# Bursts of three score tiles, a new order of MLP units, transposed constants and earlier first scores in a fused attention and MLP kernel

## The chip, the cores and the metric

The kernel runs on one core of a Trainium2 chip. The metric is the device time of one execution in microseconds (us), as a median over several runs. A difference of less than 2% counts as "same" in the verdicts, so most of what follows is about differences that need many rounds on the same chip, or the trace, to be seen at all. A "cold" stretch is one in which the trace shows a granted TensorE clock of 0.50.

## The reference

For 8 batches of 12 heads, 448 positions and head size 64: q and k are normalized by their root mean square and scaled by gains, then softmax attention; its output, 3584 tokens of 768, goes through an MLP with a leaky activation whose slope `alpha` differs per hidden unit.

```python
q_n, k_n = rmsnorm(q, g_q), rmsnorm(k, g_k)
scores = np.matmul(q_n, k_n.transpose(0, 1, 3, 2)) / sqrt(64)
attn = softmax(scores)                      # over keys
x = matmul(attn, v) -> (3584, 768)
h = x @ w_in                                # 768 x 2048
g = np.maximum(h, 0.0) + alpha * np.minimum(h, 0.0)
out = g @ w_out                             # 2048 x 768
```

## The kernel before

The kernel is scheduled by hand: the order in which instructions are written is the order on each engine. A batch is three blocks `y` of four heads, a block is seven score tiles `j`. The engines are called as in the profile: PE is TensorE, DVE is VectorE, ACT is ScalarE, POOL is GpSimd. One block's life:

- POOL squares q and k (`square`), DVE sums the squares (`reduce`), ACT makes 1/root (`root`), POOL scales (`scale`; DVE for the first blocks), PE transposes both and DVE copies them out of PSUM, the memory into which PE writes (`turn`);
- PE makes score tiles (`score`), ACT their exponential (`soft`), PE sums over keys with ones (`den`), ACT inverts by a logarithm and an exponential (`log`, `invert`), PE multiplies with v (`attv`) and DVE multiplies by the inverse into `xT`;
- the MLP of a batch is 16 "up" units of six matmuls and about seven "down" units of sixteen matmuls.

```python
def turn(y):
    ps = psa.tile([128, 2, 512], FP32, name="tps", tag="acc")     # one buffer, shared with den and attv
    ...  # 7 transposes of q, 7 of k, then one copy each
def attv(y):
    av = over_keys("av", y, lambda g, par, j: vv[...])            # 28 matmuls of 64x64, tag "acc"
    nc.vector.tensor_mul(out=xT[b][:, :, i, :], in0=av[:, :, :S], in1=rden[y])
def up(b, ft):
    hT = psf.tile([128, 512], FP32, name="hT", tag="mm")          # two buffers, shared with down
    ...  # six matmuls
    nc.scalar.activation(out=ah, in_=hT[:, :S], func=AF.Copy, scale=alpha_sb[:, ft : ft + 1])
    nc.vector.tensor_max(out=gT[:, ft, ds((b & 1) * S, S)], in0=hT[:, :S], in1=ah)
```

The program is a row of bursts. Each has two score tiles, possibly a denominator or an attention product, possibly a turn, then the MLP units that a planner put into its gap.

```python
    for b in range(1, B):
        at(J * G * b / 2 - 4, load_v, b)        # the second batch's v: burst 6
    ...
    for c in range(4):
        load_w_in(c)
        at(8 + 2 * c, load_w_out, c)            # bursts 8, 10, 12, 14
    ...
    for n in range(NB + 2):
        for f, a in prep.get(n, ()):
            f(*a)
        tiles = [divmod(m, J) for m in (2 * n, 2 * n + 1) if m < NG * J]
        for t in tiles:
            score(*t)
        if n in dens:
            den(dens[n])
        if n in avs:
            attv(avs[n])
        ...   # softmaxes, logarithm, root and scale of a later block
        if n in turns:
            turn(turns[n])
        for f, a in gaps[n]:                    # up and down units
            ...
        if n < first:
            spin(4 if plain else 1)             # matmuls that only fill PE's gaps
```

## Time and profile before

The median was 482.68 us of three runs.

| Stage of the trace | PE | ACT | What sets the pace |
|---|---|---|---|
| 0 to 14 us | filling matmuls | waits for q and k | the first loads |
| 14 to 50 us (head, no MLP work yet) | about 80% | about 85% | ACT |
| 50 to 450 us | about 97% | about 60% | PE |

In the profile, a busy share says when an engine had work and not how well it was used. Costs on PE are therefore read from the starts of successive groups in the timeline. The prediction shows the lines.

### The profile page before, as it was taken

Reading aid. Unit: us, or ns where it says so; the run is one execution under the profiler, and the core shown is the slowest. Engines: PE = TensorE matmul, PEld = TensorE weight load, DVE = VectorE, ACT = ScalarE, POOL = GpSimd, SP = SyncE. Lnnn points to the kernel's source line nnn. Section 1 sums busy time; section 2 is a strip of 40 time slices with the busy share of each in tenths; the row PEclk is TensorE's granted clock in tenths of the full one; section 3 lists DMA queues with packets and bytes.
Section 4 is the critical chain, followed back from the end, with each engine's and each line's share of the span. In section 5 each row is a group of like instructions: output and inputs, shape, how many; then the busy total and the mean of one; then the engine's idle time right before and its main releaser. Section 6 shows DMA issues by size and latency. Waiting matters only on the chain.

```text
span 480.6 us, 9494 instructions
## 1 busy us (share of the span) xinstructions
PE 451.2 (94%) x4074; PEld 234.9 (49%) x4074; DVE 217.3 (45%) x312; ACT 289.1 (60%) x399; POOL 167.0 (35%) x123
## 2 busy tenths in 40 slices
PE   7777899999999999999999999999999999999995
PEld 3243444555455445555545554554545554555463
DVE  2843564545354445355453454454462443334421
ACT  4788789567756657656755757548674558423300
POOL 4688734554253261451442351532623200000000
PEclk9799999999999999999999999999999999999998
DMA  7999997340705243431704434423401110111122
GB/s 197 200 266 221 241 209 135 110 110 3 167 1 143 77 116 53 117 100 38 167 0 110 110 100 69 110 54 90 92 1 35 34 34 1 34 34 33 34 65 67
DMA packets 32187, 45.46 MB, mean 95 GB/s; under 512 B 5008, under 2 KB 28560, under 8 KB 32144
## 3 DMA queue, kind: packets, MB, share of 16 engines
q1 hardware_dynamic: 19792, 32.13, 25.8%
q0 software_dynamic: 11776, 11.80, 15.7%
q10 hardware_dynamic: 576, 0.92, 0.7%
q8 instruction: 32, 0.52, 0.5%
q14 instruction: 11, 0.09, 0.1%
HBM read 45.62 MB, written 11.01 MB: 118 GB/s over the span
## 4 chain that ended last, share of the span: by engine, by line
PE 70%; ACT 12%; DVE 9%; issue 4%; POOL 3%; DMA 1%; SPq 0%; POOLq 0%; DVEq 0%; ACTq 0%
PE op L266 30%; PE hT L249 20%; ACT ah L257 6%; PE sc L189 6%; PE av L212 6%; PE dn L212 4%; DVE gT L258 4%; ACT expT L201 4%; DVE ss L133 3%; PE tps L166 2%; DMA nat<-in_k_dram 1%; POOL qs L150 1%; POOL sq L127 1%; ACT rden L227 1%; PE spin L289 1%
## 5 line engine op out<-in xcount | busy, mean ns | idle before, releaser
L201 ACT ACTIVATE expT<-sc,expb 128x896 f16<-128x896 f32 x168 | 160.4, 1004 | 51.2 <-PE sc L189 51.1
L249 PE MATMUL hT<-xT,w_in_sb 128*128 128x448 f16 x768 | 159.9, 352 | 8.1 <-DVE gT L258 6.5
L266 PE MATMUL op<-w_out_sb,gT 128*128 128x384 f16 x896 | 153.3, 326 | 1.7 <-DVE gT L258 1.7
L257 ACT ACTIVATE ah<-hT,alpha_sb 128x448 f16<-128x448 f32 x128 | 80.7, 635 | 97.2 <-PE hT L249 96.2
L258 DVE TENSOR_TENSOR gT<-hT,ah 128x448 f16<-128x448 f32 x128 | 79.5, 624 | 123.5 <-ACT ah L257 123.3
L150 POOL TENSOR_TENSOR qs<-nat,rr 128x896 f16<-128x896 f32 x45 | 75.0, 1688 | 127.9 <-ACT rr L145 104.1
L266 PEld LDWEIGHTS <-gT 128*128 128x128 f16 x896 | 85.2, 98 | 64.3 <-issue 11.2
L249 PEld LDWEIGHTS <-w_in_sb 128*128 128x128 f16 x768 | 72.4, 97 | 86.0 <-issue 26.2
L127 POOL TENSOR_TENSOR sq<-nat 128x896 f32<-128x896 f32 x44 | 72.9, 1677 | 85.4 <-DVE ss L133 85.4
L278 DVE COPY osb<-op 128x384 f32<-128x384 f32 x56 | 31.1, 556 | 86.5 <-PE op L266 86.5
L189 PE MATMUL sc<-qT,kT 64*64 64x448 f16 x672 | 51.7, 370 | 9.9 <-DVE kT L176 4.5
L133 DVE TENSOR_REDUCE ss<-sq 128x14 f32<-128x896 f32 x48 | 49.8, 1076 | 7.0 <-ACT sq L125 7.0
L240 DVE TENSOR_TENSOR xT<-av,rden 128x896 f16<-128x896 f32 x24 | 26.2, 1092 | 29.9 <-PE av L212 29.9
L212 PE MATMUL av<-expT,vt 64*64 64x448 f16 x672 | 36.0, 349 | 1.3 <-ACT rden L227 1.3
L212 PE MATMUL dn<-expT,ones 64*64 64x448 f16 x672 | 35.9, 349 | 0.0
L189 PEld LDWEIGHTS <-kT 64*64 64x64 f16 x672 | 13.9, 105 | 42.7 <-issue 32.2
L212 PEld LDWEIGHTS <-vt 64*64 64x64 f16 x672 | 20.0, 107 | 13.6 <-issue 2.4
L212 PEld LDWEIGHTS <-ones 64*64 64x64 f16 x672 | 19.9, 107 | 11.8 <-issue 0.3
L166 PE MATMUL tps<-ident,qs 128*128 128x128 f16 x336 | 23.3, 220 | 1.9 <-POOL qs L150 1.6
L227 ACT ACTIVATE rden<-dn 128x896 f32<-128x896 f32 x24 | 22.1, 921 | 3.5 <-PE dn L212 3.5
L166 PEld LDWEIGHTS <-qs 128*128 128x128 f16 x336 | 18.8, 98 | 10.8 <-issue 5.6
L232 ACT ACTIVATE rden<-rden 128x896 f32<-128x896 f32 x24 | 22.6, 943 | 0.3
(25 smaller groups left out, 98.9 us busy)
## 6 DMA issues: line engine op xcount, KB each, us to landing
out_dram<-osb SPq DMA_DIRECT2D x56, 192.0 KB, 2.7
nat<-in_q_dram SPq DMA_DIRECT2D x46, 224.0 KB, 3.8
nat<-in_k_dram SPq DMA_DIRECT2D x46, 224.0 KB, 4.6
vt<-in_v_dram POOLq DMA_DIRECT2D x16, 336.0 KB, 5.5
w_in_sb<-in_moe_w_in_dram POOLq DMA_DIRECT2D x4, 768.0 KB, 19.0
w_out_sb<-in_moe_w_out_dram POOLq DMA_DIRECT2D x4, 768.0 KB, 16.2
nat<-in_q_dram ACTq DMA_DIRECT2D x2, 224.0 KB, 5.2
nat<-in_k_dram ACTq DMA_DIRECT2D x2, 224.0 KB, 7.1
```

Of the source, the lines that this page charges most:

```text
L127: nc.gpsimd.tensor_mul(out=sqf, in0=src, in1=src)
L133: nc.vector.tensor_reduce(out=ss_t[y][:, "qk".index(nm)].rearrange("p h j -> p (h j)").unsqueeze(2), in_=sqs[y, nm], axis=AXIS_X, op=ALU.add,)
L150: eng.tensor_mul(out=t.rearrange("p j h d -> p h j d"), in0=nat[y, nm], in1=rr_t[y][:, "qk".index(nm)].unsqueeze(3).broadcast_to((128, 2, ...
L166: nc.tensor.transpose(tp[:, j, :], qs[y, nm][:, j].rearrange("p h d -> p (h d)"), ident)
L189: nc.tensor.matmul(out=sc[ds(64 * g, 64), par, :S], lhsT=kT[ds(64 * par, 64), g, j, :], rhs=qT[ds(64 * par, 64), g].rearrange("p j c -> p ...
L201: nc.scalar.activation(out=expT[y][:, j], in_=scs[y, j][:, :, :S], func=AF.Exp, scale=QK_SCALE, bias=expb[:, 0:1],)
L212: nc.tensor.matmul(out=acc[ds(64 * par, 64), g, :S], lhsT=weights(g, par, j), rhs=e[ds(64 * g, 64), j, par, :], start=(j == 0), stop=(j == ...
L249: nc.tensor.matmul(out=hT[:, :S], lhsT=w_in_sb[:, c, ts(ft, 128)], rhs=x[:, c, :], start=(c == 0), stop=(c == KM - 1),)
L257: nc.scalar.activation(out=ah, in_=hT[:, :S], func=AF.Copy, scale=alpha_sb[:, ft : ft + 1])
L258: nc.vector.tensor_max(out=gT[:, ft, ds((b & 1) * S, S)], in0=hT[:, :S], in1=ah)
L266: nc.tensor.matmul(out=op[:, :OH], lhsT=gT[:, ft, ts(t, 128)], rhs=w_out_sb[:, ft, ds(oh * OH, OH)], start=(ft == 0), stop=(ft == NF - 1),)
L278: nc.vector.tensor_copy(out=o[:, ds(oh * OH, OH)], in_=op[:, :OH])
```

## The change

The intent is to let PE change less often between score work and MLP work, to keep third MLP units in a row from waiting for PSUM, and to start the first scores earlier. The diff, cut to its core:

```diff
@@ constants: rows, then one PE transpose, in place of 4-byte loads @@
+    rows = cst.tile([NF + 2, 128], FP32, name="rows", tag="rows")
+    cols = cst.tile([128, NF + 2], FP32, name="cols", tag="cols")
+    alpha_sb = cols[:, :NF]
@@ load_qk: the second block's loads wait for ACT @@
+            if hold and nm == "q":
+                nc.scalar.copy(out=t[:, 0, 0, 0:1], in_=expb)
@@ square @@
-        sq = ld.tile([128, 2 * J, D], FP32, name="sq", tag="sq", bufs=2)
+        sq = ld.tile([128, 2 * J, D], FP32, name="sq", tag="sq", bufs=4)
@@ turn: own PSUM tile for the first k; layout (j, g, c) in place of (g, j, c) @@
+        ps2 = psf.tile([128, 512], FP32, name="tps2", tag="mm") if y == 0 else ps[:, 1]
-            t = att.tile([128, 2, J, 64], FP16, name=f"{nm}T", tag=f"{nm}T", bufs=3)
+            t = att.tile([128, J, 2, 64], FP16, name=f"{nm}T", tag=f"{nm}T", bufs=3)
@@ plan of the bursts @@
+        if len(dens) > len(avs):
+            avs[n] = len(avs)
+        elif len(dens) < NG and last_in.get(len(dens), n) < n:
+            dens[n] = len(dens)
+        wide = n in dens and dens[n] >= G or n in avs and avs[n] >= G - 1
+        count = min(3 if wide else 2, NG * J - m)
@@ loads and preparation @@
-        at(J * G * b / 2 - 4, load_v, b)
+        at(av_at[G * b] - 4, load_v, b)          # the second batch: burst 11
-        at(8 + 2 * c, load_w_out, c)
+        at(7 + c, load_w_out, c)
@@ units: a down may now open any burst; a burst with a turn has two units @@
-            free = n in avs or n in turns
+            free = True
+                short = n in turns and len(gaps[n]) < 2
@@ start: q's chain before k's; gains multiplied between @@
-    spin(34)
+    spin(22)
+    ct = psf.tile([128, 512], FP32, name="ct", tag="mm")
+    nc.tensor.transpose(ct[:, : NF + 2], rows, ident32[: NF + 2, : NF + 2])
+    spin(12)
@@ main loop @@
-        for t in tiles:
+        for t in tiles[:2]:
             score(*t)
 ...  # den or attv
+        for t in tiles[2:]:
+            score(*t)
+            soft(*t)
 ...
-        if n in turns:
-            turn(turns[n])
         for k, (f, a) in enumerate(gaps[n]):
 ...
+            if k == 0 and n in turns:
+                turn(turns[n])
-            spin(4 if plain else 1)
+            spin(4)
```

More of the change, by code (lines that the diff above doesn't have):

```diff
@@ L76 @@
     nc.vector.memset(idle, 0.0)
+    ident32 = cst.tile([32, 32], FP32, name="ident32", tag="ident32")
+    make_identity(nc, ident32)
+    rows = cst.tile([NF + 2, 128], FP32, name="rows", tag="rows")
+    cols = cst.tile([128, NF + 2], FP32, name="cols", tag="cols")
+    alpha_sb = cols[:, :NF]
     gain = cst.tile([128, 1], FP32, name="gain", tag="gain")
-    gk2 = cst.tile([128, 1], FP32, name="gk2", tag="gk2")
-    alpha_sb = cst.tile([128, NF], FP32, name="alpha_sb", tag="alpha_sb")
     w_in_sb = cst.tile([128, KM, DF], FP16, name="w_in_sb", tag="w_in_sb")
@@ L85, with load_qk @@
     SRC = {"q": q4, "k": k4}
-    def load_qk(y):
+    def load_qk(y, hold=False):
         b, i = divmod(y, G)
@@ L159, in turn @@
         ps = psa.tile([128, 2, 512], FP32, name="tps", tag="acc")
+        ps2 = psf.tile([128, 512], FP32, name="tps2", tag="mm") if y == 0 else ps[:, 1]
         tps = [
-            ps[:, n, : S].bitcast(FP16).rearrange("p (j c) -> p j c", j=J)
-            for n in range(2)
+            t[:, : S].bitcast(FP16).rearrange("p (j c) -> p j c", j=J)
+            for t in (ps[:, 0], ps2)
         ]
@@ L169, in turn @@
         for tp, nm in zip(tps, "qk"):
-            t = att.tile([128, 2, J, 64], FP16, name=f"{nm}T", tag=f"{nm}T", bufs=3)
-            o = t.rearrange("p g j c -> p j g c")
-            i4 = tp.rearrange("p j (g c) -> p j g c", g=2)
+            t = att.tile([128, J, 2, 64], FP16, name=f"{nm}T", tag=f"{nm}T", bufs=3)
+            o = t.rearrange("p j g c -> p j (g c)")
             if nm == "q":
-                nc.vector.tensor_copy(out=o, in_=i4)
+                nc.vector.tensor_copy(out=o, in_=tp)
             else:
                 nc.vector.tensor_scalar(
-                    out=o, in0=i4, scalar1=gain[:, 0:1], scalar2=None, op0=ALU.mult
+                    out=o, in0=tp, scalar1=gain[:, 0:1], scalar2=None, op0=ALU.mult
                 )
@@ L189, in score @@
                 nc.tensor.matmul(
-                    out=sc[ds(64 * g, 64), par, :S],
-                    lhsT=kT[ds(64 * par, 64), g, j, :],
-                    rhs=qT[ds(64 * par, 64), g].rearrange("p j c -> p (j c)"),
+                    out=sc[ds(64 * g, 64), par, :S].rearrange("p (j c) -> p j c", j=J),
+                    lhsT=kT[ds(64 * par, 64), j, g, :],
+                    rhs=qT[ds(64 * par, 64), :, g, :],
                     start=True,
@@ L291, in spin @@
                 )
-    NB = (NG * J + 1) // 2
-    def last(y):
-        return (J * y + J - 1) // 2
-    dens = {last(y) + 1: y for y in range(NG)}
-    avs = {last(y) + 2: y for y in range(NG)}
+    bursts, dens, avs, first_in, last_in = [], {}, {}, {}, {}
+    m = 0
+    while m < NG * J or len(avs) < NG:
+        n = len(bursts)
+        if len(dens) > len(avs):
[4 more added lines that the diff above has]
+        count = min(3 if wide else 2, NG * J - m)
+        bursts.append([divmod(m + c, J) for c in range(count)])
+        for y, j in bursts[n]:
+            first_in.setdefault(y, n)
+            if j == J - 1:
+                last_in[y] = n
+        m += count
+    NB = len(bursts)
+    den_at = {y: n for n, y in dens.items()}
+    av_at = {y: n for n, y in avs.items()}
     prep, post, roots = {}, {}, {}
@@ L309, in after @@
         post.setdefault(max(int(n), 0), []).append((f, a))
-    turn_at = [J * y // 2 - 1 for y in range(NG)]
-    turns = {n: y for y, n in enumerate(turn_at) if y}
+    turn_at = {
+        y: max(n for n in range(first_in[y]) if n not in dens) for y in range(1, NG)
+    }
+    turns = {n: y for y, n in turn_at.items()}
     jobs = {}
     for y in range(G, NG):
-        n = turn_at[y - 1] if y < G + 2 else last(y - G) + 2
-        at(n - 8, load_qk, y)
+        early = y < G + 2
+        n = turn_at[y - 1] if early else max(d for d in dens if d <= turn_at[y] - 2)
+        at(n - (8 if early else 5), load_qk, y)
         for nm in "qk":
             at(n - 2, square, y, nm)
-            if y < G + 2:
+            if early:
                 after(n, reduce, y, nm)
@@ L338 @@
         ]
-        tail = len(new) if b == B - 1 else 2 + odd
+        tail = len(new) if b == B - 1 else 2 if odd or b == 0 else 1
         periods.append((ups, carry, new[:tail]))
@@ L343, in cost @@
     def cost(n):
-        return 0.75 + (1.35 if n in dens or n in avs else 0.0) + (0.9 if n in turns else 0.0)
-    first = last(G - 1) + 2
-    gaps = [[] for _ in range(NB + 2)]
+        return (
+            0.31 + 0.19 * len(bursts[n])
+            + (1.35 if n in dens or n in avs else 0.0) + (0.9 if n in turns else 0.0)
+        )
+    first = av_at[G - 1]
+    gaps = [[] for _ in range(NB)]
     for b in range(B - 1):
-        lo = last(G * b + G - 1) + 2
-        hi = last(G * b + 2 * G - 1) + 2
+        lo, hi = av_at[G * b + G - 1], av_at[G * b + 2 * G - 1]
         ups, old, new = (list(u) for u in periods[b])
@@ L368 @@
                 ahead = 0.5 * (UP if ups else DOWN)
-                if n < hi - 1 and clock + ahead > per * (n - lo + 1):
+                short = n in turns and len(gaps[n]) < 2
+                if n < hi - 1 and not short and clock + ahead > per * (n - lo + 1):
                     break
@@ L381 @@
     nc.scalar.preload_act_table_set("natural_log_exp_and_others")
-    for g in range(2):
-        nc.gpsimd.dma_start(out=gain[ds(64 * g, 64)], in_=g_q.unsqueeze(1))
-        nc.gpsimd.dma_start(out=gk2[ds(64 * g, 64)], in_=g_k.unsqueeze(1))
-    load_qk(1)
+    nc.gpsimd.dma_start(out=rows[:NF], in_=moe_alpha.rearrange("(t p) -> t p", p=128))
+    for n, g in enumerate((g_q, g_k)):
+        for h in range(2):
+            nc.gpsimd.dma_start(
+                out=rows[NF + n : NF + n + 1, ds(64 * h, 64)], in_=g.unsqueeze(0)
+            )
+    load_qk(1, True)
     load_qk(2)
-    nc.sync.dma_start(out=alpha_sb, in_=moe_alpha.rearrange("(t p) -> p t", p=128))
-    spin(34)
+    spin(22)
+    ct = psf.tile([128, 512], FP32, name="ct", tag="mm")
+    nc.tensor.transpose(ct[:, : NF + 2], rows, ident32[: NF + 2, : NF + 2])
+    spin(12)
     for nm in "qk":
@@ L392 @@
         reduce(0, nm)
-    for nm in "qk":
         root(0, nm)
         scale(0, nm)
-    nc.vector.tensor_mul(out=gain, in0=gain, in1=gk2)
+        if nm == "q":
+            nc.vector.tensor_copy(out=cols, in_=ct[:, : NF + 2])
+            nc.vector.tensor_mul(
+                out=gain, in0=cols[:, NF : NF + 1], in1=cols[:, NF + 1 : NF + 2]
+            )
     turn(0)
@@ L411 @@
     roots[3] = 2
-    for n in range(NB + 2):
+    for n in range(NB):
         for f, a in prep.get(n, ()):
             f(*a)
-        tiles = [divmod(m, J) for m in (2 * n, 2 * n + 1) if m < NG * J]
-        for t in tiles:
+        tiles = bursts[n]
+        for t in tiles[:2]:
             score(*t)
+        plain = n not in dens and n not in avs
+        wait = plain and gaps[n] and gaps[n][0][0] is up
+        for t in tiles[:1] if wait else tiles[:2]:
+            soft(*t)
         if n in dens:
@@ L422 @@
             attv(avs[n])
-        plain = n not in dens and n not in avs and n not in turns
-        wait = plain and gaps[n] and gaps[n][0][0] is up
+        for t in tiles[2:]:
+            score(*t)
+            soft(*t)
         late = []
-        for t in tiles[:1] if wait else tiles:
-            soft(*t)
         if wait:
@@ L432 @@
             log(dens[n])
-            late = [(2, invert, (dens[n],))]
+            if gaps[n] and gaps[n][0][0] is down:
+                invert(dens[n])
+            else:
+                late = [(1, invert, (dens[n],))]
         if n in roots:
@@ L438 @@
                 scale(y, nm)
-        if n in turns:
-            turn(turns[n])
         done = 0
-        for f, a in gaps[n]:
+        for k, (f, a) in enumerate(gaps[n]):
             if f is down:
@@ L451 @@
                     late = []
+            if k == 0 and n in turns:
+                turn(turns[n])
+        if not gaps[n] and n in turns:
+            turn(turns[n])
         for _, g, c in late:
```

## The prediction

> **What bounds the kernel now.** I read the page's busy table first, then the 40 slices, the sums over stretches of time, the waits, and last the timeline of one steady stretch and of the start.
>
> ```profile
> span 480.6 us, 9494 instructions
> PE 451.2 (94%) x4074; PEld 234.9 (49%) x4074; DVE 217.3 (45%) x312; ACT 289.1 (60%) x399; POOL 167.0 (35%) x123
> ...
> PE   7777899999999999999999999999999999999995
> PEclk9799999999999999999999999999999999999998
> ```
>
> TensorE (PE) is the bound, at 94%, and its first four slices are the loosest; the second slice (12 to 24 us) also has a lower clock. The sums over stretches separate the stages:
>
> ```profile
> 12.00:20.00 8.00, 6.31 (x42) 1.92 (x39) 6.30 (x8) 4.95 (x7) 5.41 (x6) 0.59 1.31 188
> ...
> 30.00:40.00 10.00, 7.04 (x109) 3.75 (x105) 4.85 (x6) 8.70 (x12) 9.02 (x8) 1.00 1.20 243
> ...
> 200.00:300.00 100.00, 97.33 (x907) 50.80 (x906) 47.22 (x68) 65.35 (x90) 35.70 (x24) 1.00 0.37 86
> ```
>
> The columns are the stretch, its length, busy PE, weight loads, DVE, ACT, POOL, then clock, DMA share and GB/s. Up to 50 us there is no MLP work and ACT sets the pace (8.70 of 10 us). From 50 us on PE sets it, at 97%. A busy PE is not an efficient one, so I take costs from start to start in the steady timeline:
>
> ```profile
> 152.82 0.57 PE L189 MATMUL sc<-qT,kT 64*64 64x448 f16 x8
> ...
> 153.33 0.96 PE L166 MATMUL tps<-ident,qs 128*128 128x128 f16 x14
> ...
> 154.12 2.76 PE L266 MATMUL op<-w_out_sb,gT 128*128 128x384 f16 x16
> ...
> 156.72 1.30 PE L249 MATMUL hT<-xT,w_in_sb 128*128 128x448 f16 x6
> ...
> 157.95 0.57 PE L189 MATMUL sc<-qT,kT 64*64 64x448 f16 x8
> ...
> 158.35 1.49 PE L212 MATMUL dn<-expT,ones 64*64 64x448 f16 x28
> ...
> 159.78 2.44 PE L249 MATMUL hT<-xT,w_in_sb 128*128 128x448 f16 x12
> ```
>
> Start to start: two score tiles take 0.51 us before the transposes and 0.40 before the denominator, 14 transposes 0.79, one down unit (16 matmuls) 2.60, one up unit (6) followed by scores 1.23, the 28 denominator matmuls followed by an up 1.43. An up followed by other work of its kind is about 1.14. So entering a score burst costs about 0.09 to 0.10, and leaving the 64x64 shape for the 128x128 one 0.11 to 0.13: **about 0.23 us fixed per burst**, whatever lies in it. The second loss is in the waits of PE (from 60 to 440 us, 9.7 us in all):
>
> ```profile
> PE hT L249 <- DVE gT L258: 5.5, 21, 0.3
> PE sc L189 <- ACT ah L257: 2.1, 4, 0.5
> PE op L266 <- DVE gT L258: 1.7, 6, 0.3
> ```
>
> These are third units in a row: the MLP has two PSUM buffers, and an up's buffer comes back only after ACT's 0.64 us and DVE's 0.62 us.
>
> **What the Trainium skill says.** "TensorEngine Tiling (Array Packing)", section Tiling Modes, Key Properties: changing the tiling mode drains TensorE. The trace agrees: the 0.10 in and 0.12 out above. "DMA: Bandwidth & Descriptors", Specifications: at least 512 B per transfer for line rate. The trace agrees: alpha, 8 KB in 4-byte pieces, lands in 6.8 us, the 0.2 KB gains in 5.3 and 6.4, a 224 KB q load in 3.8. "VectorE: DVE Perf Modes", section What auto-detection actually checks: the two-per-cycle mode needs 16-bit tensors with step 1. The old copies have that in runs of 64, and the trace says they run in it: 896 elements in 622 ns (q) and 675 (k), against 1076 for a 896-element fp32 reduction. So I expect contiguous copies to **save nothing** on DVE. "TensorE: Matmul & The Clock Gate", Part 1: an idle window halves the clock. The stretch 12 to 20 us at 0.59 agrees; there four idle-filling matmuls take 1.68 us instead of about 0.8.
>
> **The change part by part.** (1) **Bursts.** Following the loops of the diff, the 168 score tiles lie in 84 bursts now and 64 after: 41 of three tiles, 22 of two, one of one. The head keeps its two-tile bursts up to the twelfth; the 20 bursts saved all lie in the PE-bound part. 20 x 0.23 = 4.6 us saved. The third tile comes after the denominator or the attention product, in the same 64x64 shape, so it adds no change of shape, but small fill costs (about 0.03 us x 41 = 1.2 us). It needs the first tile's PSUM buffer: PE arrives 0.40 + 1.31 = 1.71 us after the burst begins; ACT frees it at about 0.43 + 1.0 = 1.43 after a down, or, with an up's activation in front, 0.74 + 1.0 = 1.74. So about 0.05 us x 25, again 1.2 us lost. Net of part 1: **-2.2**.
>
> (2) **Order of MLP units.** In the new plan nearly every burst begins with a down when one is there, and turns fall between the first and second unit, which separates ups. In the plan from burst 34 to 48, two batches, I count five third-in-a-row waits of about 0.4 us, one row of five (0.8 in place of one of these) and one of about 1.35 where three softmaxes and a logarithm (3.9 us of ACT) stand before an up: about 3.8 us. The same two batches now: 55.91 + 54.96 = 110.9 us between the starts of attention products, less 2 x 50.6 of work (16 x 1.14 + 7 x 2.60 + 21 x 0.187 + 6 x 1.31 + 3 x 0.79), less 21 x 0.23 = 4.8 fixed, leaves 4.9. So 1.1 saved per two batches, about **-3** over six. The first batch with MLP is nearly ACT-bound (38 us of ACT against 40 of PE, 43.7 taken) and gains perhaps 0.5; the tail alternates one more down with the last ups, 0.3 to 0.5: **-1** together. The longer carry of down units only moves work.
>
> (3) **The start.** Now:
>
> ```profile
> 8.38 0.95 ACT L125 ACTIVATE sq<-nat 128x896 f32<-128x896 f32 x1 [2.31 <-DMA nat<-in_k_dram]
> ...
> 11.06 1.43 DVE L150 TENSOR_TENSOR qs<-nat,rr 128x896 f16<-128x896 f32 x1 [0.62 <-ACT rr L145]
> ...
> 13.69 0.67 DVE L176 TENSOR_SCALAR kT<-tps,gain 128x896 f16<-128x896 f16 x1
> ...
> 14.42 0.96 PE L189 MATMUL sc<-qT,kT 64*64 64x448 f16 x8 [1.31 <-DVE kT L176]
> ```
>
> Everything waits for the first k, at 8.3 us. The hold keeps the second pair's loads back until ACT has loaded its table (3.4 us), and the 4-byte gain pieces go, so k should land near 6. But the new ACT order puts q's root (which waits for q's reduction, over at 7.2) before k's square: the square starts at about 7.75, not 8.38, so **0.65** is saved there. The own PSUM tile lets q's copy run beside k's transposes: 0.55 saved. If q also lands 0.3 us earlier, that adds 0.3. First score at about 13.0: **-1.4**. The transpose of rows and the copy of 18 columns are short and beside other work; the same 34 warming matmuls remain.
>
> (4) **The rest of the head.** From 14.4 to 49.4 us ACT has 26 softmaxes x 0.95, three pairs of logarithm and exponential x 1.86 and four roots x 0.55 = 32.5 of 35 us. Four square buffers in place of two remove POOL's waits for the reduction (0.98 us near 33 us), the second v load leaves POOL's way, two w_out issues of 0.8 enter it; the third turn then no longer waits for POOL (0.5). I put **-0.8**; more filling matmuls may shorten the cold stretch, or not.
>
> Sum: -2.2 - 3 - 1 - 1.4 - 0.8 = -8.4 us; I allow 0.5 back for ACT's burstier load: 482.7 - 7.9, about **474.8 us**, 1.6% less.
>
> **Rivals.** (a) ACT becomes the bound in bursts: a wide denominator burst has three softmaxes and the logarithm before the next up, 3.9 us, where PE has only 2.1 us before that up. For it: the first MLP batch. Against it: ACT has 65% over the steady part, and most wide bursts put a 2.60 us down first. Each wide burst losing 0.2 us would give back 8 us: 482. (b) The fixed cost per burst is really larger, 0.3 as the new plan's own constant says (0.31 + 0.19 per tile), and the waits go nearly all: 20 x 0.31 + 7 + 4 in the head = 17: 466 us. For it: the author's constants seem fitted; against it: my start-to-start differences, which agree to 0.01. (c) The early gain is hidden, since the weights or POOL, not the first score, set when MLP work starts; then 476.5. Against it: ACT has little slack from 15 to 49 us. (d) The strided moving operand (runs of 64) makes score matmuls slower; nothing in this trace shows such a read. 0.1 us x 168 tiles would cost 17 us: 492.
>
> **Range and chances.** The start and head are known to about 1.5 us, the waits to 3, rival (a) has one chance in five, (b) one in seven, (d) one in thirty. Eight in ten: 469.5 to 479.5. The 2% line lies at 473.0, 1.8 below my number, so: faster 0.32, same 0.65, slower 0.03.
>
> **What would show it.** Bursts: 64 entries to score rows, scores' busy time below 51.7 us by some 3 to 5. Start: first score near 13.0 and first up near 47.3. Copies: still 620 and 675 ns; if clearly shorter, I misread their mode. Third tile: PE's waits for the softmax under 2 us after 60 us; if they exceed 5, rival (a). Waits of ups and downs for gT: from 8.2 us down to about 5 to 6. Attention products of two steady batches: 110.9 us now, about 108.5 after. I am wrong if the steady batches do not shorten, or if PE's busy share there stays and the score row grows.

## More of the kernel before

The kernel before takes some 481 to 484 us.

Loads and POOL's work are hung on burst numbers; the loads of v, `w_in` and `w_out` all go through the queue of POOL.

## The result, and the profile after

The changed kernel took 485.21 us (484.90 to 485.96, four runs) against 483.04 (482.49 to 484.44, four runs): **0.4% slower**, ratio 1.0043 with a 95% interval of 1.0018 to 1.0068. A ratio here is the mean time of one kernel's runs over that of the other's from the same rounds, so it is not quite the ratio of the quoted medians. The prediction said 474.8 and a range up to 479.5.

The page of the changed kernel, its span, busy times and the rows of the 40 slices for PE and its clock:

```profile
span 484.2 us, 9569 instructions
...
PE 453.2 (94%) x4099; PEld 243.9 (50%) x4099; DVE 218.0 (45%) x313; ACT 289.3 (60%) x400; POOL 167.8 (35%) x126
...
PE   8898959899989999899999999899999999999996
...
PEclk9899988999999999999999999999999999999998
```

The head is fuller than before (8s and 9s in place of 7s). But the sixth slice, 60.5 to 72.6 us, has fallen from 9 to 5, and the clock dips beside it. The timeline of PE there, with columns start, length, engine, line, operation, count and the idle time before it:

```profile
62.71 0.57 PE L196 MATMUL sc<-qT,kT 64*64 64x448 f16 x8
67.73 0.38 PE L219 MATMUL av<-expT,vt 64*64 64x448 f16 x2 [4.45 <-DMA vt<-in_v_dram]
69.40 2.82 PE L219 MATMUL av<-expT,vt 64*64 64x448 f16 x26 [1.29 <-DMA vt<-in_v_dram]
71.64 0.95 PE L196 MATMUL sc<-qT,kT 64*64 64x448 f16 x4
72.53 2.42 PE L256 MATMUL hT<-xT,w_in_sb 128*128 128x448 f16 x6
```

The attention product, which normally follows two score tiles by 0.40 us, waits 5.7 us for v. After that the clock has dropped: 26 matmuls take 2.82 us, and an up unit 2.2 from start to start where 1.14 is usual. The chain of waits says when this v was asked for (start, length, what):

```profile
46.33 1.70 POOL qs L157
48.03 0.64 POOL vt L109
48.67 20.68 DMA vt<-in_v_dram
...
69.40 2.82 PE av L219 x21
```

The load left at 48 us and landed 20.7 us later. That it took so long is not what changed. The views of `vt`, the tile of v, in the changed kernel and then in the kernel before show the same longest landing:

```profile
DMA to landing us min/median/max: 4.4/8.2/20.7
```

```profile
DMA to landing us min/median/max: 4.2/5.5/20.6
```

In the kernel before this load (its second half) left at 32.5 us, behind the four `w_in` loads, and landed at 53.1, well before its attention product at 61.9.

In the steady part the change did what it was to do. Two steady batches, six attention products from start to start, took 110.87 us and take 108.83 us: 2.0 us less, where the prediction had 2.4 (108.5). The stretch from 200 to 300 us looks as before:

```profile
200.00:300.00 100.00, 97.71 (x954) 54.55 (x954) 48.66 (x70) 65.97 (x91) 35.39 (x23) 1.00 0.34 82
```

PE's busy share there cannot show the gain: it is 97% either way, and only the amount of work done in the stretch differs (954 matmuls in place of 907).

### The profile page after: what moved, and what is told of

Its sections match the earlier page's. It is cut to its first block, busy times and chain, and to the rows that moved or that the text cites. A ratio compares the mean times of both kernels' runs of the same rounds, so it can differ in the third digit from the quotient of the medians.

```text
span 484.2 us, 9569 instructions
## 1 busy us (share of the span) xinstructions
PE 453.2 (94%) x4099; PEld 243.9 (50%) x4099; DVE 218.0 (45%) x313; ACT 289.3 (60%) x400; POOL 167.8 (35%) x126
## 4 chain that ended last, share of the span: by engine, by line
PE 69%; ACT 10%; DVE 7%; DMA 6%; issue 3%; POOL 3%; SPq 0%; POOLq 0%; ACTq 0%
PE op L273 31%; PE hT L256 18%; PE sc L196 6%; PE av L219 5%; ACT ah L264 5%; PE dn L219 4%; DMA vt<-in_v_dram 4%; ACT expT L208 4%; DVE gT L265 4%; PE tps L174 3%; DMA nat<-in_k_dram 2%; PE spin L296 2%; POOL qs L157 1%; DVE ss L140 1%; DVE kT L183 1%
## 5 line engine op out<-in xcount | busy, mean ns | idle before, releaser
L208 ACT ACTIVATE expT<-sc,expb 128x896 f16<-128x896 f32 x168 | 157.8, 1007 | 25.8 <-PE sc L196 25.4
L264 ACT ACTIVATE ah<-hT,cols 128x448 f16<-128x448 f32 x128 | 81.3, 635 | 134.2 <-PE hT L256 133.5
L196 PE MATMUL sc<-qT,kT 64*64 64x448 f16 x672 | 54.5, 367 | 5.7 <-DVE kT L183 3.4
L219 PE MATMUL av<-expT,vt 64*64 64x448 f16 x672 | 37.7, 358 | 6.4 <-DMA vt<-in_v_dram 5.7
L196 PEld LDWEIGHTS <-kT 64*64 64x64 f16 x672 | 18.6, 105 | 37.3 <-issue 25.4
L174 PEld LDWEIGHTS <-qs 128*128 128x128 f16 x336 | 20.9, 99 | 7.9 <-issue 3.8
```

Source lines behind the costliest of these rows:

```text
L174: nc.tensor.transpose(tp[:, j, :], qs[y, nm][:, j].rearrange("p h d -> p (h d)"), ident)
L196: nc.tensor.matmul(out=sc[ds(64 * g, 64), par, :S].rearrange("p (j c) -> p j c", j=J), lhsT=kT[ds(64 * par, 64), j, g, :], rhs=qT[ds(64 * ...
L208: nc.scalar.activation(out=expT[y][:, j], in_=scs[y, j][:, :, :S], func=AF.Exp, scale=QK_SCALE, bias=expb[:, 0:1],)
L219: nc.tensor.matmul(out=acc[ds(64 * par, 64), g, :S], lhsT=weights(g, par, j), rhs=e[ds(64 * g, 64), j, par, :], start=(j == 0), stop=(j == ...
```

## The experiments

Twelve kernels ran, all with a correct result. Those whose name begins with a, c or d start from the changed kernel, those with b from the kernel before. They ran in four sets of rounds on different chips (a and b_late; c; d and b_start; b_start4), and the changed kernel's own times come from yet another set. The kernel before differs by about 1 us in median from set to set, so figures that compare runs of different sets are read from medians and from the spans of the traces together. In the traces I read "the third product" as the start of the attention product of block 2, which ends the head, the sixth as that of block 5, which ends the first MLP batch, and the last as that of block 23.

### Was it the late v?

The first kernel, a_v_early, puts only v back to burst 6:

```diff
-        at(av_at[G * b] - 4, load_v, b)
+        at(6 if b == 1 else av_at[G * b] - 4, load_v, b)
```

> The changed kernel with one edit: the second batch's v load is asked for at burst 6 again, as before, not at burst 11. Theory (late v): the 5.7 us wait of the attention product for v near 63 us and the half-clock stretch after it vanish, the third attention product of batch two starts near 63 us in place of 67.7, and the time falls by 8 to 10 us to 475 to 477.5. Rival (the bursts themselves overload ACT): the wait only changes its name, to the softmax or the logarithm, and the time stays above 482. Rival (DMA is full up to 60 us, whatever the order): another load, w_out or q and k, comes late in its place, and the time lies between, 479 to 482.

Measured 479.04 us against 482.28 of the kernel before in the same rounds, ratio 0.9936 (0.9919 to 0.9952). The wait for v is gone from PE's waits. The time falls by about 6 us, but not to the expected 475 to 477.5: something else must be missing too. (The next two runs also end a little above what was expected of them.)

The second, a_wout_slow, leaves v at burst 11 and puts the `w_out` loads back to their old pace:

```diff
-        at(7 + c, load_w_out, c)
+        at(8 + 2 * c, load_w_out, c)
```

> The changed kernel with one edit: the four w_out loads are asked for at bursts 8, 10, 12, 14 as before, and v stays at burst 11. If it is the w_out loads ahead of v in the queue that delay it, v has two w_out loads ahead of it and not four, lands about 8 to 10 us earlier (near 60) and most of the wait goes: 476 to 478. If v is late only because it is asked for at 48 us, it lands as late as before: 484 to 486.

Measured 478.65 us, ratio 0.9927 (0.9912 to 0.9941), and no wait for v either. So asking at 48 us was not too late by itself. It was too late behind all four `w_out` loads, which in the changed kernel left at 34.0, 39.1, 43.1 and 43.9 us on the same queue; the old pace leaves two of them for later, and v, asked for at 47.6 us, lands at 61.5, 1.2 us before it is needed. The Trainium skill, "DMA: Bandwidth & Descriptors", section Queues, rings and completion order, says that a queue row has its own ring on each of the sixteen engines, that an engine consumes descriptors in ring order, and that it takes turns only between rows. That agrees with the landings here: the four `w_out` loads at 49.5, 55.0, 60.4 and 66.4 us, then v at 69.4.

The third, a_both, has both edits, and so the loads of this queue in the order of the kernel before:

```diff
-        at(av_at[G * b] - 4, load_v, b)
+        at(6 if b == 1 else av_at[G * b] - 4, load_v, b)
-        at(7 + c, load_w_out, c)
+        at(8 + 2 * c, load_w_out, c)
```

> The changed kernel with both edits, so the order of all loads on this queue is that of the kernel before. Late-v theory: the same time as with v early alone, within 1 us (475 to 477.5), unless the two w_out issues of 0.8 us each in the head cost something on GpSimd, then up to 1 us faster. Rival: no better than 482.

Measured 478.60 us, ratio 0.9926 (0.9911 to 0.9941), the same as either alone. This is the mended kernel of the rest of this section.

The fourth, b_late, brings the changed order of loads alone into the kernel before:

```diff
-        at(J * G * b / 2 - 4, load_v, b)
+        at(11 if b == 1 else J * G * b / 2 - 4, load_v, b)
-        at(8 + 2 * c, load_w_out, c)
+        at(7 + c, load_w_out, c)
```

> The kernel before with the changed order of loads alone: v of the second batch at burst 11, w_out at bursts 7 to 10. Late-v theory: the kernel before stalls too; its attention product that starts at 61.9 us waits for v until some 68 us, and with a colder clock behind it the time rises by 5 to 9 us to 488 to 492. Rival (the stall comes from the bursts): no change, 482 to 484.

Measured 495.57 us, ratio 1.0270 (1.0245 to 1.0296), more than expected. PE's waits from 60 to 440 us have a new first line:

```profile
PE av L212 <- DMA vt<-in_v_dram: 5.9, 2, 3.5
PE hT L249 <- DVE gT L258: 5.3, 20, 0.3
```

The wait for v is as long as in the changed kernel. The rest is in the head, where the third product starts at 50.14 us in place of 47.94 (two more `w_out` issues stand before POOL's scaling, and the transposes wait 2.2 us for it), and in two cold stretches, at 41 and 69 us, of 6.8 us each; their shares are not separated. The stall therefore belongs to the order of loads and not to the bursts.

### Where the other 4 us are

The mended kernel is 3.8 us above the prediction. The starts of the attention products divide its trace and that of the kernel before (spans 476.8 and 480.6 us):

| Stretch | Before | Mended | Difference | Predicted |
|---|---|---|---|---|
| head, to the third product | 47.94 | 45.87 | -2.1 | -2.2 |
| first MLP batch, to the sixth (two score tiles of 0.19 us more) | 43.72 | 46.88 | +3.2, or +2.8 without these tiles | -0.5 |
| to the last product (one down unit of 2.6 us and these two tiles fewer) | 330.37 | 323.25 | -4.5 without that unit, or -4.1 without the tiles too | -5.2 |
| tail (that unit more) | 58.60 | 60.76 | -0.4 without that unit | -0.3 to -0.5 |

The differences sum to -3.8, the difference of the spans. (The counts of matmuls in each stretch show the work that moved.) One stretch is wrong: the first batch with MLP work. The first rival says that wide bursts overload ACT there. So c_two takes them away altogether:

```diff
-        wide = n in dens and dens[n] >= G or n in avs and avs[n] >= G - 1
+        wide = False
```

> The kernel with both load edits (v at burst 6, w_out at 8 to 14), and bursts of two tiles everywhere, planned by the new planner. By the prediction's part 1 the 20 bursts more cost 20 x 0.23 = 4.6 us and save 2.4 us of third-tile costs: two steady batches take about 110.3 us in place of 108.8, and by that alone the whole is 2.2 us slower, 480.8. Against it the first MLP batch, which took 46.9 us with wide bursts and 43.7 before, should come back to about 44; then the two nearly cancel: 477.5 to 479.5, steady batches slower and the first one faster. Rival (wide bursts gain nothing anywhere): two steady batches stay below 109 us and the whole falls to 476.

Measured 479.50 us against 483.35, ratio 0.9918 (0.9906 to 0.9931). By the ratios that cannot be told apart from the mended kernel's 0.9926; by medians (478.60) and spans (477.6 against 476.8) it is 0.9 us slower. So the times alone leave open what wide bursts are worth. The traces do not: two steady batches take 110.18 us with bursts of two and 108.83 with bursts of three, in both pairs. Six bursts less at 0.23 us are 1.38, which fits the fixed cost per burst that the prediction read from the starts. The first batch takes 45.39 us with bursts of two and 46.88 with three. Of these 1.5 us, 0.4 are the two score tiles more, so 1.1 us of the loss come with wide bursts. The other 1.7 are there without them: the transposes of two blocks wait 0.60 and 1.01 us for POOL's scaling.

```profile
66.80 0.56 PE L174 MATMUL tps<-ident,qs 128*128 128x128 f16 x7 [0.60 <-POOL qs L157]
...
84.86 0.56 PE L174 MATMUL tps<-ident,qs 128*128 128x128 f16 x7 [1.01 <-POOL qs L157]
```

The edit does more than its name says. Run through the plan's loop, it also moves the transposes: with bursts of two, 19 of the 21 blocks that it places have their turn one burst after their root, and none has it in a burst with an attention product; with bursts of three the turn is two or three bursts after the root, and for 20 of the 21 it stands in such a burst.

Next, c_first keeps bursts of two in the first batch only.

```diff
-        wide = n in dens and dens[n] >= G or n in avs and avs[n] >= G - 1
+        wide = n in dens and dens[n] >= 2 * G or n in avs and avs[n] >= 2 * G - 1
 ...  # and two roots in one burst where the plan now asks for it
```

> The same kernel with bursts of two in the first MLP batch and of three only from the second on, where down units exist. If wide bursts hurt only where no down unit stands in front of the next activation, the first batch returns to about 44 us and the steady ones stay at 108.8 per two: 475.5 to 476.5. If the first batch's loss has another cause (the place of the turn, say), it stays near 47 and the time near 478.6.

Measured 480.13 us, ratio 0.9939 (0.9927 to 0.9952): a miss. Its first batch takes 47.06 us. The edit was not clean. The plan now prepares blocks 7 and 8 at the same burst, so POOL gets their squares together, and the transposes wait 3.1 us for POOL's scaling over the run. It tells nothing on wide bursts.

What holds the first batch up shows in the waits of PE in the mended kernel, from 50 to 440 us (who waits for whom: us in total, times, longest). Of the second line, 2.2 us lie in the first batch and 1.1 in one burst of the second:

```profile
PE hT L256 <- DVE gT L265: 5.7, 19, 1.0
PE tps L174 <- DVE xT L247: 3.3, 3, 1.1
...
PE sc L196 <- ACT expT L208: 1.4, 2, 0.8
```

The transposes wait for the multiply that frees their PSUM tile. And this multiply waits on its own engine (DVE's timeline):

```profile
64.13 0.62 DVE L265 TENSOR_TENSOR gT<-hT,ah 128x448 f16<-128x448 f32 x1 [0.74 <-ACT ah L264]
64.67 2.07 DVE L140 TENSOR_REDUCE ss<-sq 128x14 f32<-128x896 f32 x2
66.66 1.08 DVE L247 TENSOR_TENSOR xT<-av,rden 128x896 f16<-128x896 f32 x1
```

Two sums of squares stand before it in program order, and it is the plan with wide bursts that puts a turn right behind this multiply. In most bursts they are issued inside a down unit, but the first batch's bursts have none. So c_red moves them behind the multiply, and the root behind the units, where there is no down unit:

```diff
         if n in avs:
             attv(avs[n])
+        moved = len(held) > 0
+        for f, a in held:          # reductions left over from the burst before
+            f(*a)
+        held = []
 ...
-        if n in roots:
+        if n in roots and not moved:
 ...  # root and scale; then the units
+        if n in roots and moved:
+            ...  # root and scale behind the units
-        for f, a in jobs.pop(n, []) + post.get(n, []):
+        held = jobs.pop(n, [])
+        for f, a in post.get(n, []):
             f(*a)
```

> The same kernel with wide bursts throughout; where a denominator burst has no down unit, the two square reductions (2.07 us on VectorE) go behind the attention product's multiply of the next burst, and the root behind the MLP units. Theory (order on VectorE): the reductions stand in front of the multiply that frees the PSUM tile which the transposes need; the transposes' waits for it, 3 x 1.1 us after 60 us, vanish and the time falls by 2 to 3.3 us to 475.3 to 476.6. Rival (ACT is the bound there): the waits move to the softmax and the time stays within 0.7 of 478.6.

Measured 477.03 us, ratio 0.9867 (0.9854 to 0.9880). That is 1.6 us below the mended kernel by medians and by spans (475.2 against 476.8), short of the 2 to 3.3 expected; the ratios of the two sets of rounds would make it 2.8. The edit moves the root and POOL's scaling too, and no run separates them from the sums. The line of the transposes' waits is gone:

```profile
PE hT L256 <- DVE gT L265: 6.1, 20, 1.0
PE sc L196 <- DVE kT L183: 2.6, 7, 0.9
PE op L273 <- DVE gT L265: 2.5, 4, 1.0
PE sc L196 <- ACT expT L208: 1.6, 3, 0.8
```

Of the 3.3 us, 1.2 return as waits of the scores for k's copy (1.4 before). The first batch takes 45.67 us, 1.2 less than in the mended kernel, and still has two of its third tiles waiting for the softmax (0.79 and 0.60 us). That much of the rival on ACT is true, in this batch.

### The start and the head

In c_gain, which starts from the mended kernel, the gains' product moves behind the first k's reduction, and the transpose of the constants six matmuls later:

```diff
-    spin(22)
+    spin(28)
     ...  # transpose of the constants
-    spin(12)
+    spin(6)
     for nm in "qk":
         square(0, nm)
         reduce(0, nm)
-        root(0, nm)
-        scale(0, nm)
-        if nm == "q":
+        if nm == "k":
             nc.vector.tensor_copy(out=cols, in_=ct[:, : NF + 2])
             nc.vector.tensor_mul(out=gain, ...)
+        root(0, nm)
+        scale(0, nm)
```

> The same kernel with the 18-column copy and the product of the gains behind the first k's reduction in place of before it, and 28 of the 34 warming matmuls ahead of the transpose of rows. Theory: the one-column product waited for the end of GpSimd's multiply (it ended at 9.7 to 9.8 us in every run, whenever it began), and the reduction behind it; the reduction now starts near 8.9, the first score near 13.1 in place of 13.9, and the time falls by 0.5 to 0.9 us. Rival (ACT's or the load's order hides it): first score earlier, time unchanged within 0.3.

The times are 478.36 us, ratio 0.9894 (0.9882 to 0.9907), within 0.3 us of the mended kernel's median from other rounds. DVE in the mended kernel first, then in c_gain (the bracket gives idle time and what ended it):

```profile
9.11 0.73 DVE L427 TENSOR_TENSOR gain<-cols 128x1 f32<-128x1 f32 x1
9.76 1.07 DVE L140 TENSOR_REDUCE ss<-sq 128x14 f32<-128x896 f32 x1
```

```profile
8.91 1.09 DVE L140 TENSOR_REDUCE ss<-sq 128x14 f32<-128x896 f32 x1 [1.46 <-ACT sq L132]
...
10.12 0.16 DVE L425 TENSOR_TENSOR gain<-cols 128x1 f32<-128x1 f32 x1
```

A product of two columns of one element took 0.73 us, up to the end of POOL's multiply at 9.8 us, and 0.16 without it. The Trainium skill, "SBUF — State Buffer", section Who interferes with whom, says that a VectorE instruction with two SBUF inputs and a GpSimd instruction that reads SBUF exclude each other for their whole length. The trace agrees. The first score starts at 13.11 us in place of 13.94, as expected, but the third product only 0.14 us earlier: the gain is hidden behind the second block's scaling on DVE, which then takes 3.15 us for two in place of 2.28, again beside POOL's squares. The rival of this run was right.

The last two kernels on the head add to the kernel before, first, only the new start (constants as rows, hold, own PSUM tile, q's chain first), its core being:

```diff
+        ps2 = psf.tile([128, 512], FP32, name="tps2", tag="mm") if y == 0 else ps[:, 1]
-    load_qk(1)
+    load_qk(1, True)
-    nc.sync.dma_start(out=alpha_sb, in_=moe_alpha.rearrange("(t p) -> p t", p=128))
+    nc.gpsimd.dma_start(out=rows[:NF], in_=moe_alpha.rearrange("(t p) -> t p", p=128))
-    spin(34)
+    spin(22)
+    ct = psf.tile([128, 512], FP32, name="ct", tag="mm")
+    nc.tensor.transpose(ct[:, : NF + 2], rows, ident32[: NF + 2, : NF + 2])
+    spin(12)
     for nm in "qk":
         square(0, nm)
         reduce(0, nm)
-    for nm in "qk":
         root(0, nm)
         scale(0, nm)
-    nc.vector.tensor_mul(out=gain, in0=gain, in1=gk2)
+        if nm == "q":
+            ...  # copy of the constants, product of the gains
```

> The kernel before with only the changed start: alpha and gains as rows, the hold, the own PSUM tile, the q chain ahead of the k chain; old copies, two square buffers, old plan and old order of loads. If the start gave the 2.1 us by which the head is shorter in the mended kernels: the third attention product starts near 45.9 in place of 47.9 and the time falls by about 2 us to 480.5 to 481.5. If the head was shortened by the square buffers, the order of loads or the filling matmuls: the first score near 13.9, but the third attention product after 47 and the time within 1 us of before.

Measured 481.43 us against 483.02, ratio 0.9964 (0.9951 to 0.9977). The first score comes at 13.86, but the third product at 47.87. The 1.6 us in the times is more than the traces show (480.1 against 480.6). The profiled run was the slowest of the five, at 481.99 us, and that of the kernel before, at 482.54, lies near the fast end of its times here (482.40 to 484.26). And a cold stretch, from 22.1 to 25.6 us, hides the start's lead in this trace. It stands right behind the scores that wait for the second block's k, and these come 0.56 us earlier (the kernel before, then b_start):

```profile
22.63 0.38 PE L189 MATMUL sc<-qT,kT 64*64 64x448 f16 x4 [0.81 <-DVE kT L176]
```

```profile
22.07 0.57 PE L195 MATMUL sc<-qT,kT 64*64 64x448 f16 x4 [0.81 <-DVE kT L182]
```

So this trace does not settle what the start alone is worth at the third product. Then four square buffers are added:

```diff
-        sq = ld.tile([128, 2 * J, D], FP32, name="sq", tag="sq", bufs=2)
+        sq = ld.tile([128, 2 * J, D], FP32, name="sq", tag="sq", bufs=4)
```

> The kernel before with the changed start and four square buffers in place of two, nothing else. The changed start alone left the third attention product at 47.87 us, where the mended kernels have it at 45.8 to 45.9. If GpSimd's squares, freed from waiting for the reductions, no longer stand against VectorE's scaling of the second pair (3.45 us for two in the run before, 2.28 in the mended kernel), the first transposes come 1 us earlier, the third attention product at 46 to 46.5, and the time falls to 479.5 to 480.5. If the head's gain comes from the filling matmuls or the order of loads instead: still near 47.8, time within 0.3 us of the start alone (481.4).

Measured 479.97 us against 482.55, ratio 0.9945 (0.9932 to 0.9958). The scaling of the second block, two instructions on DVE, in the start alone and then with four buffers:

```profile
16.70 3.45 DVE L155 TENSOR_TENSOR qs<-nat,rr 128x896 f16<-128x896 f32 x2 [0.91 <-ACT rr L150]
```

```profile
16.85 2.61 DVE L155 TENSOR_TENSOR qs<-nat,rr 128x896 f16<-128x896 f32 x2 [0.91 <-ACT rr L150]
```

With two buffers POOL's squares wait for the sums and then run just when DVE scales; with four, one of them is over before. The scores behind the second block's k start at 21.39 us, 0.68 us earlier than in the start alone; the first product comes at 26.59 in place of 27.76, with the cold stretch above in the difference. The third product, at 47.35, is later than expected. This run, the slowest of six by 1.3 us, has a cold stretch at 32 us, which may be why; no trace of a run without one was kept.

### A better version

The kernel d_all joins a_both, c_red and c_gain. Its diff is the sum of theirs:

```diff
+        at(6 if b == 1 else av_at[G * b] - 4, load_v, b)      # a_both
+        at(8 + 2 * c, load_w_out, c)                          # a_both
+        held = jobs.pop(n, [])                                # c_red
+        if nm == "k":                                         # c_gain: constants before k's root
```

> The candidate for the best version: both load edits, the reductions behind the attention product's multiply where no down unit stands in the burst, and the product of the gains behind the first k's reduction. If the gains add: the reductions' 1.6 us and at most 0.3 from the start, 476.6 to 477.2, 1.2 to 1.4% below the kernel before.

Measured **476.75 us** (476.54 to 476.77) against 483.02, ratio 0.9864 (0.9847 to 0.9881): within what was expected. It beats the kernel before by 1.4% and, by the medians of different rounds, the changed kernel by 1.7%. To see there what bursts of three are worth, d_two takes them away on the same chip:

```diff
-        wide = n in dens and dens[n] >= G or n in avs and avs[n] >= G - 1
+        wide = False
```

> The candidate with bursts of two tiles everywhere, on the same chip in the same rounds. It tells what bursts of three are worth by themselves: from the steady batches of the runs already made (110.2 us per two against 108.8) 1.35 x 3 = 4 us less what the first batch and the tail give back. If bursts of three help by more than they cost: 0.8 to 3 us slower than the candidate. If they are worth nothing: within 0.5 us of it.

Measured 498.61 us, ratio 1.0313 (1.0297 to 1.0330). That is far outside what was expected, and it is no answer on the bursts. PE's waits have this as their first line:

```profile
PE tps L174 <- POOL qs L157: 15.3, 15, 1.3
```

In the plan with bursts of two, a block is transposed in the burst after its root. The edit of c_red pushes the root to the end of its burst, so POOL's scaling comes too late for almost every block. With bursts of three there are one or two more bursts between. The better comparison remains that of c_two with a_both.

## Why the prediction was wrong

**The step that failed first** is in the prediction's part 4: "the second v load leaves POOL's way, two w_out issues of 0.8 enter it". Both moves were counted only as time on POOL's instruction stream. What they do to the landing of v was not asked. The v load left 16 us later, stood behind four `w_out` loads, and cost 6.2 to 6.6 us (485.2 against 478.6 to 479.0; 7 us between the third and the sixth product in the traces), shown by undoing either move, and by b_late, where the order of loads alone makes the kernel before 2.7% slower. None of the four rivals was this one; (c) came nearest, with loads that hide the early gain.

**The second** is in part 2: "The first batch with MLP is nearly ACT-bound ... and gains perhaps 0.5". It lost 3.2 us, 0.4 of them two score tiles that moved into it. The size came from sums of work per engine, which say nothing on the order within one. c_red takes 1.2 us of it away by the order on DVE (the two reductions, moved with the root); c_two has 1.7 us of it without any wide burst, beside 1.6 us of waits of the transposes for POOL. The 1.1 us of wide bursts and the 1.2 us of reductions probably overlap, since it is the wide plan that puts the transposes behind that multiply; no run separates them, and they are not to be added. What is left after c_red, 45.67 against 43.72 us with the two tiles more, is 1.5 us. PE waits there 1.9 us for k's copy and 1.8 for the softmax; the cause is not settled further.

**What held:**

- Part 1, the fixed cost of 0.23 us per burst: 1.35 us measured for six bursts. Of the costs put on the third tile, the fill cost of 0.03 us was not there. From start to start a wide denominator burst takes 0.402 + 1.324 + 0.292 = 2.02 us, against 0.403 + 1.427 = 1.83 with two tiles, so the third costs 0.19, its bare work. The wait for the softmax, put at 1.2 us, was 1.4 after 60 us, but in two waits of the first batch. The net of the whole part against c_two, equal work taken, is -2.1 us from the sixth product to the end and +1.1 in the first batch: -1.0 where -2.2 was predicted.
- Part 2 in the steady batches: with bursts of two, 110.87 fell to 110.18 us per two batches, 0.7 where 1.1 was predicted. The tail gained 0.4 as said.
- Part 3, the start: -0.6 us at the first score, not -1.4. The step "first score at about 13.0" missed the gains' product, which waits for POOL; c_gain then reached 13.1. (k landed at 7.6 us, not "near 6", but its square began at 7.85, close to the 7.75 of the sum.) And the 0.83 us that c_gain gained at the first score were worth 0.14 at the third product, in traces with no cold stretch. So rival (c), a hidden early gain, was right there, though what hid it was DVE's scaling beside POOL's squares. What the start as a whole is worth stays open: 1.6 us by the times of b_start, 0.07 at the third product of its trace, which a cold stretch disturbs.
- Part 4's remainder, -0.8: the head as a whole came out as predicted (-2.1 against -2.2), but not by the predicted parts. The scores behind the second block's k gained 0.56 us by the start and 0.68 by the square buffers (b_start, b_start4). Some 0.6 us arise between the first and the third product (20.11 us before, 19.51 in the mended kernel); whether by the filling matmuls, the order of work or the clock was not tested.
- The copies still take 623 ns and 676 ns, as the prediction said of their mode. So the contiguous layout saved nothing on DVE, and the strided operand of rival (d) cost nothing (two score tiles before a denominator still take 0.40 us).

**Two readings that misled.** The prediction took the cold stretch before 20 us as agreeing with the page's idle window, but no gap of PE there was longer than 1.3 us (see the last section). And it named the busy time of the score row as a test: it should fall by 3 to 5 us from 51.7, and the prediction was wrong if it grew. It grew to 54.5 (53.3 in the mended kernel, which has no cold stretch there) while the steady batches became shorter. The row counts the modelled end of each group's last matmul; a third tile standing alone, whose group takes 0.36 us in the timeline and 0.29 from start to start, adds such an end.

## What to carry to other kernels

When a change moves a load, first ask when it lands and what stands before it in its queue, and only then what its issue costs the engine; a load that was hidden can stop the bound engine, and here the clock was cold for 6.8 us after it. Count costs of PE from start to start, and check a plan's order on every in-order engine: two reductions in front of a multiply that frees a PSUM tile went with 1.6 us here, nearly as much as two steady batches gained. When a trace is one run, look where its cold stretches lie before reading a small difference from it. An earlier start is worth only what the next link of the chain lets through.

## What the Trainium skill lacked or had wrong

- "TensorE: Matmul & The Clock Gate" gives the rule of no idle gaps over about 3.4 us. It also says that frequent short gaps can lower the clock and that transposes do not count as busy in the same way, but has no figure for either. In the kernel before the clock was at half from 13.45 to 20.27 us, with no gap of PE longer than 1.31 us near its start; in the 3.41 us before it PE was busy for 1.63, of which 1.13 in transposes. b_start4 turned cold at 32.1 us after 1.77 busy (0.95 in transposes) and gaps of at most 1.12. No threshold comes out of these runs: c_first was busy for 1.70 from 10.10 to 13.51 us and kept its clock.
- "TensorEngine Tiling (Array Packing)" says that a change of tiling mode drains TensorE, but has no figure for it. From start to start, going into the 64x64 tiles took 0.09 to 0.10 us here and out of them 0.11 to 0.13, 0.23 per burst.
- "DMA: Bandwidth & Descriptors" has no figure for a load behind others of its queue: 20.7 us behind four `w_out` loads here and 20.6 behind four `w_in` loads in the kernel before, against a median of 8.2 and a least of 4.4 us for the same size in the changed kernel.
- "SBUF — State Buffer" has the exclusion between VectorE and GpSimd, but no case of the smallest operand: a 128x1 product took 0.47 to 1.03 us under it, 0.15 to 0.16 without.
